# Spreading scale vectors by VectorE's stream shuffle and moving one batch's q load, in a fused attention and MLP kernel

## The chip, the cores and the metric

One core of a Trainium2 chip. The metric is the time of one execution on the device in microseconds. Every kernel was timed against the kernel before on the same chip in the same rounds. "The profile" is one profiled execution, with times from the start of its span (some 1.7 us shorter than the timed execution).

## The reference, cut to what matters

```python
# 8 batches, 16 q heads, 4 kv heads, 384 tokens, head size 64, so d_model = 1024
attn = softmax(q @ k.T / 8) @ v                 # then x: (8, 384, 1024)
a1 = alpha1 * x + beta1                         # vectors over d_model
u  = x + lam * einsum('ts,bsd->btd', w_tok, a1)
a2 = alpha2 * u + beta2
out = u + lam * (maximum(a2 @ w_ch1, 0) @ w_ch2)   # w_ch1 1024x4096, w_ch2 4096x1024
```

The kernel keeps w_ch2 in SBUF from the first batch on and streams w_ch1 (8 MB in bf16) anew for each batch. For each batch there are two channel passes: the first multiplies by w_ch1 (16 chunks of two 128-column tiles, matmuls "h"), the second by w_ch2 (matmuls "ch"). The attention of batch b+1 is woven into the second pass of batch b; that of batch 0 stands alone in the first 38 us, the attention stage.

## The kernel before: what the change and the argument touch

Four vectors of 1024 (alpha1 x lam, beta1 x lam, alpha2, lam) have to stand in all 128 partitions, in `vecs`. They come as rows of 32x128, are split into bf16 parts, and a PE matmul with a 0/1 weight adds the parts and spreads the sum:

```python
def spread(ps_, vs, tag, eng="DVE"):
    n = len(ps_)
    ps = bank([P, 4, P], tag, "vec")
    w = vs[1] - vs[0]
    for i, p in enumerate(ps_):
        nc.tensor.matmul(out=ps[:, i * w:(i + 1) * w], lhsT=sel[:, p:p + 1].to_broadcast([P, P]),
                         rhs=rows_b[:, vs[0] * P:vs[1] * P], start=True, stop=True)
    evac(eng)(out=vecs[:, vs[0]:vs[1], ...], in_=ps[:, :n * w]...)        # cut
```

The start, in GpSimd's order of issue (w1 tiles turn into bf16 on the way; a ring of five):

```python
load_v(0); load_q4(2); nc.gpsimd.dma_start(out=wtok_in, ...); load_q4(3)
place_k(0, 0, (0,))
load_w1(0); load_w1(1)
place_k(0, 1)
scale_rows(1, nc.gpsimd); split(1, 2, None, nc.gpsimd)
for c in range(2, RING):
    load_w1(c)
load_k(1); load_q(1); load_v(1)
for i in range(3):
    load_w2(0, i, 8)
for f in side(0):          # attention stage of batch 0
    f()
```

The end of the first channel pass, and where the third batch's q goes:

```python
if b or c + RING < NCH:
    load_w1(b * NCH + c + RING)          # tile of five chunks later
...
if b == 0 and c == NCH - 1:
    for i in range(RING):
        load_w1(NCH + i)
    load_next(2)                         # place_k(2), load_q(2), load_v(2)
...
moves = [(0, 1, flip_k, 2), (0, 1, flip_q, 2, 0, 2)] if b == 1 else []   # turns by DMA
turns = {16 + 8 * i: [(q_transpose, 2 + 2 * i, 2, "three")] for i in range(3)} if b == 2 else {}   # turns by PE
```

`side(b)` and `turns` hold what is woven in, by the number of steps that a pass has done (in the first pass four to a chunk, but two to each of the first two chunks of the first batch). A turn is a transposition, by DMA or by PE; a2T is the turned a2, which the matmuls "h" read. "tok" are the matmuls over w_tok, and R, in the tile `stage`, is a weight that they use in the first batch, made from the sums over w_tok.

The softmax here doesn't subtract the row's maximum and nothing guards it: scores larger than these inputs give would overflow.

## Time and profile before

| | before |
|---|---|
| median of the timed runs | 803.76 us (3 runs, 802.71 to 803.96) |
| profiled span | 802.3 us |
| PE busy | 790.1 us, 98% |
| first matmul of channel pass 1 of batch 0 (PE timeline) | 37.70 us |
| first matmul of its pass 2 | 77.61 us |
| first matmul of pass 1 of batch 1 | 132.66 us |
| first matmul of its pass 2 | 176.03 us |

The last four rows are milestones. They are starts of the first L414 or L447 matmul after the other one in PE's timeline.

### The profile page before, as it was taken

Reading aid. Unit: us, or ns where it says so; the run is one execution under the profiler, and the core shown is the slowest. Engines: PE = TensorE matmul, PEld = TensorE weight load, DVE = VectorE, ACT = ScalarE, POOL = GpSimd, SP = SyncE. Lnnn points to the kernel's source line nnn. Section 1 sums busy time; section 2 is a strip of 40 time slices with the busy share of each in tenths; the row PEclk is TensorE's granted clock in tenths of the full one; section 3 lists DMA queues with packets and bytes.
Section 4 is the critical chain, followed back from the end, with each engine's and each line's share of the span. In section 5 each row is a group of like instructions: output and inputs, shape, how many; then the busy total and the mean of one; then the engine's idle time right before and its main releaser. Section 6 shows DMA issues by size and latency. Waiting matters only on the chain.

```text
span 802.3 us, 14186 instructions
## 1 busy us (share of the span) xinstructions
PE 790.1 (98%) x6074; PEld 454.0 (57%) x6141; DVE 344.1 (43%) x667; ACT 226.6 (28%) x308; POOL 182.2 (23%) x241
## 2 busy tenths in 40 slices
PE   8999999999999999999999999999999999999997
PEld 5765555655556555565555655566555655556545
DVE  7652555226542256323662235622365225552122
ACT  7624331232412243123221234122431223312100
POOL 9234231342013500135002340033300330003000
PEclk9999999999999999999999999999999999999999
DMA  9999999998279962999339991499914994139511
GB/s 192 202 190 202 202 206 171 206 198 114 63 138 185 198 91 62 163 191 196 69 72 174 190 194 44 96 174 198 161 47 114 170 198 85 47 65 188 78 40 40
DMA packets 232575, 112.58 MB, mean 140 GB/s; under 512 B 81976, under 2 KB 226368, under 8 KB 232512
## 3 DMA queue, kind: packets, MB, share of 16 engines
q0 software_dynamic: 170752, 83.47, 78.9%
q1 hardware_dynamic: 61216, 27.81, 14.0%
q8 instruction: 48, 0.79, 0.4%
q10 hardware_dynamic: 544, 0.39, 0.2%
q14 instruction: 15, 0.12, 0.0%
HBM read 170.53 MB, written 12.58 MB: 228 GB/s over the span
## 4 chain that ended last, share of the span: by engine, by line
PE 96%; DVE 2%; issue 1%; DMA 1%; ACT 0%; SPq 0%
PE h L414 41%; PE ch L447 40%; PE sc L217 4%; PE sc L252 4%; PE sc L275 3%; DMA a2T<-a 1%; PE h L168 1%; PE tp L203 1%; PE tok L275 0%; PE av L252 0%; PE warm L464 0%; PE ut L292 0%; DVE x L258 0%; DVE x L282 0%; PE vec L332 0%
## 5 line engine op out<-in xcount | busy, mean ns | idle before, releaser
L447 PE MATMUL ch<-w,hT 128*128 128x512 bf16 (+2 forms) x1533 | 346.1, 370 | 4.4 <-issue 1.1
L414 PE MATMUL h<-a2T,w 128*128 128x384 bf16 (+1 forms) x2016 | 331.9, 326 | 0.5 <-DMA a2T<-a 0.4
L414 PEld LDWEIGHTS <-w 128*128 128x128 bf16 x2016 | 196.8, 98 | 130.2 <-issue 0.9
L134 POOL DMA_DIRECT2D w<-in_moe_w_ch_dram x128 | 112.2, 877 | 527.1 <-PE h L414 508.6
L447 PEld LDWEIGHTS <-hT 128*128 128x128 bf16 x1600 | 144.7, 98 | 152.6 <-issue 10.1
L226 ACT ACTIVATE es<-sc 128x1024 bf16<-128x1024 f32 x126 | 121.4, 1023 | 187.7 <-PE sc L217 178.8
L424 DVE TENSOR_SCALAR hT<-h,bias 128x384 bf16<-128x384 f32 x128 | 79.1, 618 | 216.0 <-PE h L414 215.4
L422 ACT ACTIVATE hT<-h,bias 128x384 bf16<-128x384 f32 x128 | 74.3, 580 | 304.6 <-PE h L414 304.0
L452 DVE TENSOR_TENSOR o<-ch,vecs 128x512 f32<-128x512 f32 (+2 forms) x50 | 33.5, 669 | 108.7 <-PE ch L447 108.7
L252 PEld LDWEIGHTS <-es 128*128 128x128 bf16 x1008 | 38.3, 97 | 13.2
L275 PEld LDWEIGHTS <-wtokT 128*128 128x128 bf16 x576 | 37.4, 98 | 12.3 <-DVE a L265 1.7
L217 PE MATMUL sc<-qT,kT 64*128 64x384 bf16 (+2 forms) x576 | 42.1, 272 | 1.3
L252 PE MATMUL sc<-v,es 128*128 128x65 bf16 x1008 | 39.8, 193 | 0.0
L257 DVE RECIPROCAL rinv<-sc 128x6 f32<-128x6 f32 x56 | 10.8, 194 | 67.4 <-PE sc L252 66.4
L282 DVE TENSOR_TENSOR x<-sc,x 128x384 f32<-128x384 f32 x56 | 31.0, 553 | 20.0 <-PE sc L275 20.0
L275 PE MATMUL sc<-a,wtokT 128*128 128x128 bf16 x504 | 37.3, 219 | 0.4
L217 PEld LDWEIGHTS <-kT 64*128 64x128 bf16 x576 | 21.7, 94 | 24.1 <-issue 19.1
L453 DVE TENSOR_TENSOR o<-o,x 128x512 f32<-128x512 f32 (+2 forms) x50 | 33.5, 671 | 1.7
L263 DVE TENSOR_TENSOR a1f<-x,vecs 128x384 f32<-128x384 f32 x56 | 31.4, 561 | 1.9
L265 DVE TENSOR_TENSOR a<-a1f,vecs 128x384 bf16<-128x384 f32 x56 | 31.4, 561 | 1.9
L286 DVE TENSOR_TENSOR a<-x,vecs 128x384 bf16<-128x384 f32 x56 | 31.3, 558 | 1.9
L258 DVE TENSOR_TENSOR x<-sc,rinv 128x384 f32<-128x384 f32 x56 | 31.2, 558 | 1.9
(80 smaller groups left out, 212.6 us busy)
## 6 DMA issues: line engine op xcount, KB each, us to landing
w<-in_moe_w_ch_dram POOLq DMA_DIRECT2D x144, 512.0 KB, 8.7
out_dram<-o SPq DMA_DIRECT2D x47, 256.0 KB, 2.2
q_raw<-in_q_dram POOLq DMA_DIRECT2D x28, 192.0 KB, 8.3
kst<-in_k_dram SPq DMA_DIRECT2D x16, 192.0 KB, 3.8
v<-in_v_dram POOLq DMA_DIRECT2D x24, 64.0 KB, 8.2
a2T<-a SPq DMA_TRANSPOSE x56, 2.3
qg<-in_q_dram POOLq DMA_DIRECT2D x3, 192.0 KB, 4.6
stage<-in_q_dram ACTq DMA_DIRECT2D x2, 192.0 KB, 3.7
```

Of the source, the lines that this page charges most:

```text
L134: nc.gpsimd.dma_start(out=t, in_=w1src[:, :, c * CW * P:(c + 1) * CW * P])
L217: nc.tensor.matmul(out=sc[:, hh, k % 4:k % 4 + n], lhsT=kT[r, sk, 2 * p // G, :], rhs=qT[r, p, st:st + n, :], start=True, stop=True)
L226: nc.scalar.activation(out=e, in_=sc, func=EXP, scale=scale_qk)
L252: nc.tensor.matmul(out=av[:, hh, sq, :], lhsT=ess[k // 4][:, m % 2, k % 4, :], rhs=vb[:, sk, hk, :], start=(sk == 0), stop=(sk == NST - 1))
L263: nc.vector.tensor_tensor(out=t, in0=x[:, :, cols(p)], in1=bc(g1, p), op=MUL)
L275: nc.tensor.matmul(out=ps[:, tt, :], lhsT=wtokT[:, st, tt * P:(tt + 1) * P], rhs=a1s[p][:, st, :], start=(st == 0), stop=(st == NST - 1 an ...
L414: nc.tensor.matmul(out=ps[:, :n], lhsT=w1[:, dt, j * P:(j + 1) * P], rhs=a2T[:, dt, :n], start=(dt == 0), stop=(dt == NDT - 1))
L422: nc.scalar.activation(out=hT[:, nt, :], in_=ps[:, :S], func=RELU, bias=c1)
L424: nc.vector.tensor_scalar(out=hT[:, nt, :], in0=ps[:, :S], scalar1=c1, scalar2=0.0, op0=ADD, op1=mybir.AluOpType.max)
L447: nc.tensor.matmul(out=ps[:, lo:hi], lhsT=hT[:, nt, ms * P:(ms + 1) * P], rhs=w2[:, nt, dw * 512 + lo:dw * 512 + hi], start=(nt == 0), sto ...
L452: nc.vector.tensor_tensor(out=o[:, lo:hi], in0=ps[:, lo:hi], in1=lam_t[:, c], op=MUL)
L453: nc.vector.tensor_tensor(out=o[:, lo:hi], in0=o[:, lo:hi], in1=x[:, ms, c], op=ADD)
```

## The change

Its intent: take the spread off PE, the bound engine, and keep the third batch's loads from delaying the last turns of batch 1. Vectors are loaded as float32 rows to partitions 0, 32, 64 and 96 and each group of 32 partitions copies its first row (`stream_shuffle`, mask 0). Cut to its core:

```diff
+        def load_vec(i, ap, lo, n):
+            nc.sync.dma_start(out=vecs[0:P:32, i, lo:lo + n], in_=bass.AP(..., ap=[[0, 4], [1, n]]))
+        def spread(i, half):
+            t = vecs[:, i, half * 512:(half + 1) * 512]
+            nc.vector.stream_shuffle(out=t, in_=t, mask=[0] * 32)
+        def scale(i, half, eng=nc.gpsimd):
+            t, m = (vecs[:, j, half * 512:(half + 1) * 512] for j in (i, 3))
+            eng.tensor_tensor(out=t, in0=t, in1=m, op=MUL)
 ...
         place_k(0, 0, (0,))
+        units = side(0)
+        for f in units[:8]:               # first scores, and spread(0, 0), spread(3, 0) on VectorE
+            f()
+        scale(0, 0)                       # GpSimd
         load_w1(0)
         load_w1(1)
         place_k(0, 1)
-        scale_rows(1, nc.gpsimd)
-        split(1, 2, None, nc.gpsimd)
-        for c in range(2, RING):
-            load_w1(c)
+        split()                           # GpSimd, one row set
+        nc.gpsimd.memset(stage[:, 2120:2824], 0.0)
+        nc.gpsimd.memset(vecs[:, 0:4:3, 512:], 0.0)
+        load_vec(0, moe_alpha1, 512, 512)
+        load_vec(3, moe_lam, 512, 512)
+        load_w1(2)
+        load_w1(3)
+        nc.gpsimd.memset(vecs[:, 1:3], 0.0)
+        load_w1(4)
         load_k(1)
+        load_vec(1, moe_beta1, 0, DM)
+        load_vec(2, moe_alpha2, 0, DM)
 ...
-              14: [(tok, 1), (ut, 0), (a1, 4)], 15: [(av, 5), ...
+              14: [(tok, 1), (spread, 0, 1), (spread, 3, 1), (scale, 0, 1, nc.vector), (ut, 0)], 15: [(a1, 4), (av, 5), ...
 ...
-                turns = {4: [(split, 2, 4, 0)], 8: [(split, 2, 4, 1)], ...   # and six PE spreads
+                turns = {4: [(spread, 1, 0)], 6: [(spread, 1, 1)], 8: [(scale, 1, 0), (scale, 1, 1), (spread, 2, 0)],
+                         10: [(spread, 2, 1)], ...
 ...
-            turns = {16 + 8 * i: [(q_transpose, 2 + 2 * i, 2, "three")] for i in range(3)} if b == 2 else {}
+            turns = {24 + 8 * i: [(q_transpose, 2 * i, 2, "three")] for i in range(4)} if b == 2 else {}
-                load_next(2)
+                place_k(2, 0)
+                place_k(2, 1)
+            if b == 1 and c in range(1, 5):
+                load_q(2, [G * (c - 1)])
+            if b == 1 and c == NCH - RING:
+                load_v(2)
-            moves = [(0, 1, flip_k, 2), (0, 1, flip_q, 2, 0, 2)] if b == 1 else []
+            moves = [(0, 1, flip_k, 2)] if b == 1 else []
```

## The prediction

> **What bounds the kernel now.** I read the page first: the busy shares, then the chain that ended last.
>
> ```profile
> PE 790.1 (98%) x6074; PEld 454.0 (57%) x6141; DVE 344.1 (43%) x667; ACT 226.6 (28%) x308; POOL 182.2 (23%) x241
> ...
> PE 96%; DVE 2%; issue 1%; DMA 1%; ACT 0%; SPq 0%
> ```
>
> The reader is to see that TensorE is the bound: busy 98% of the span, 96% of the chain. So the change can win only (a) PE instructions it takes away and (b) the few microseconds in which PE stands. The second view is the waits, for PE alone; these are all of them but those of its warm-up and issue.
>
> ```profile
> PE ch L447 <- DVE o L452: 0.9, 2, 0.5
> PE vec L332 <- DVE hT L540: 0.6, 1, 0.6
> PE h L414 <- DMA a2T<-a: 0.4, 1, 0.4
> ```
>
> The change touches the last two. The third view is the chain in order of time, at the start, where the scale rows are split into bf16 parts before PE may spread them:
>
> ```profile
> 8.99 1.03 DVE hT L534
> 10.02 0.02 issue
> 10.05 0.37 DVE hT L540
> 10.42 0.05 issue
> 10.46 0.40 PE vec L332 x4
> ```
>
> From 6.9 to 10.5 us the chain runs over VectorE's split, a real 3.6 us. But ScalarE's exponentials run beside it: the timeline shows them back to back from 8.15 to 11.00 and from 11.25 to 18.8 us, with 0.25 us between. The split is therefore not 3.6 us of loss.
>
> The fourth view is the timeline of PE in the first channel pass. It gives the price of a spread, the distance from one start to the next:
>
> ```profile
> 58.65 1.47 PE L414 MATMUL h<-a2T,w 128*128 128x385 bf16 x8
> 59.96 0.38 PE L332 MATMUL vec<-hT,stage 128*128 128x256 bf16 x2
> 60.18 2.78 PE L414 MATMUL h<-a2T,w 128*128 128x385 bf16 x16
> ```
>
> A spread there costs 60.18 - 59.96 = 0.22 us. Last I looked at what could newly bind, the transfers. These are GpSimd's timeline near the start and the issues of w1 tiles (512 KB each) to landing, for 37.5 to 38.2 us (the sixth tile, number 5) and 157 to 170 us (second batch's first pass):
>
> ```profile
> 7.10 1.82 POOL L134 DMA_DIRECT2D w<-in_moe_w_ch_dram  x2
> 13.89 2.74 POOL L134 DMA_DIRECT2D w<-in_moe_w_ch_dram  x3
> 37.83 1.75 POOL L134 DMA_DIRECT2D w<-in_moe_w_ch_dram  x2 [7.80 <-PE h L168]
> ...
> w<-in_moe_w_ch_dram POOLq DMA_DIRECT2D x1, 512.0 KB, 7.4
> ...
> w<-in_moe_w_ch_dram POOLq DMA_DIRECT2D x5, 512.0 KB, 8.1
> ```
>
> The page's slices show the DMA at 9 tenths and about 200 GB/s from the start to 120 us. In the second batch's first pass it moves 197 GB/s with w1 alone: 524 KB / 197 = 2.66 us for a tile, where PE uses one up in 2.60 us. So in these two passes the DMA is as full as PE, and only the ring of five tiles hides it.
>
> **What the Trainium skill says.** "VectorE: DVE Perf Modes", the perf-mode tier table: STREAM_SHUFFLE has only the 1x mode, some 2400 ns at 2048 elements. The same page's errata section gives (N+151)/0.96 ns for a float32 tensor_tensor, 691 ns at 512; the trace agrees (L452, 128x512 float32, median 691 ns). My estimate for a shuffle of 128x512 from these is 0.69 us; no run yet shows one. "GPSIMD Engine Reference", 3.1: a float32 tensor_tensor of 2048 takes 4497 ns on GpSimd; a quarter of that is 1.1 us, plus start-up I take 1.3 us for 128x512. The trace has only a 32x128 one, 0.45 to 0.57 us, which doesn't contradict it. "DMA: Bandwidth & Descriptors", "Issuing engines are not separate DMA queues": transfers issued from different engines share the same DMA engines, so a transfer moved to another place still takes from w1's. The trace agrees: with two k loads on the other queue at 138 us, landing of w1 went from 7.6 to 8.6 us.
>
> **The change part by part.**
>
> 1. *Spreads off PE.* In the first pass six spreads go: 6 x 0.22 = **-1.3 us**, wholly on the path if weights arrive. In the attention stage of batch 0 two go at 0.33 us (10.46 to 10.79, 19.32 to 19.65), and the 0.6 us wait before the first. There, PE waits for exponentials anyway. I add up ScalarE's gaps that the new order can close: 0.25 at 11.0, 0.28 at 18.8, 0.48 at 21.4, together about -1.0 us.
>
> 2. *VectorE instead.* At the start two shuffles (1.4 us) replace row scaling and split (6.89 to 10.42, about 2.9 us of work), and two PSUM copies (0.67 each) go. But at about 23 us two shuffles and a scale, 3 x 0.69 less overlap = 1.9 us, stand ahead of normalisations and the tok evictions. VectorE has no idle time from 20 to 26 us; with the 0.67 copy gone the delay is some 1.2 us, of which PE, with two buffers in PSUM, feels about 0.7. Stage sum: about -0.3 us. In the first pass four shuffles (2.8 us) take the place of 1.8 us of splitting; VectorE waits 1.4 to 2 us for PE in each chunk, so they are free.
>
> 3. *GpSimd's order.* GpSimd now waits for VectorE's shuffles (end about 8.2 us), scales (1.3 us), and only then issues the first two w1 tiles: 9.5 instead of 7.1 us. Next come the k copies (1.0), the row split (4.1 us in the old timeline, 9.76 to 13.89) and two new memsets. From the old 128x128 and 128x32 memsets (0.23 and 0.12 us) one element costs 1.15 ns, so 704 + 1024 elements take about 2.2 us. The third w1 tile is issued at about 18.8 instead of 13.9 us. The first two have landed by 19.0 (7.10 + 9.2 and 7.98 + 11.0), partly earlier now since the next batch's k loads also move behind the new small loads. The DMA, which never rested here, stands still for **2 to 3 us**. All later tiles shift by that. The sixth tile landed at 37.83 + 7.4 = 45.2 us and chunk 5 began at 45.85 (PE timeline: chunk 4 begins at 42.9 after four times 8 matmuls of 0.163 us from 37.7, plus 16 matmuls and one turn of 0.33): slack 0.65 us. So PE waits, and relative to before it is late by 2 to 3 less 0.65, **+2.0 us** taken. This swallows the gain of the attention stage: whatever PE wins before chunk 5, the tile's landing sets it. Later tiles had 0.7 to 2.2 us of slack, enough for the 1.3 us of part 1.
>
> 4. *q and v of the third batch* leave the first batch's second channel pass, where the last a2T turn waited behind them: the PE wait on a2T of 0.36 to 0.44 us goes, **-0.4 us**. They come to the second batch's first pass as four q loads of 192 KB behind tiles 6 to 9: about 1.0 us each at 190 to 197 GB/s, 4.1 us. The turn by DMA (some 0.9 us there, mostly before the tiles) goes; a fourth turn on PE comes, 16 matmuls apart as before: 0.33 us (144.48 to 144.81), **+0.3 us**. Slack of w1 in this pass, from issue plus landing against the start of the chunk: tile 6 1.4 us, tile 9 2.0, tile 10 149.83 + 8.5 = 158.3 against 160.2, about 2 (tiles numbered from 0 in the pass). The dips of the DMA between 138 and 142 us take in some 0.8. Left: 4.1 - 2 - 0.8, **+1.2 us** of PE wait around chunks 9 to 11.
>
> Sum: at chunk 5 +2.0 (stage 1 to 3), -1.3, -0.4, +0.3, +1.2 = **+1.8 us**. I shade it to +1.4, since the memsets and GpSimd's scale are only estimated: 805.2 us.
>
> **The rivals.** *A, the DMA keeps up.* If GpSimd is quicker than I think, or the rings hold enough, the attention stage may gain 0.65 (the slack of the sixth tile caps it), then -1.3, -0.4 and +0.3: -1.7, and 802.1 us. For it speaks that PE never waited for a w1 tile in the old trace; against it the 197 GB/s and the 0.65 us. *B, the weights bind more.* The DMA gap of 3 us and the whole 4.1 us of q beyond 2 of slack come through: +2.4 at chunk 5 and +2.1 in the second pass, with -1.4: +3.1, and 806.9 us; with a late upper half of the scale vectors (its load waits for the GpSimd memset, and VectorE waits in order) about 1 more, 808. *C, VectorE becomes the bound of the attention stage*: if a shuffle takes twice the estimate, four of them add 2.8 us to a stage in which it has no slack, perhaps 1.5 us at the end of the stage, but hidden under the same tile wait.
>
> **Range and chances.** A is the lower edge, B with the late half the upper: 802.0 to 808.0. 2% is 16 us, over twice anything above; only a wait that recurs in every batch could do it, and batches 3 to 7 are untouched. Faster 0.005, within 2% 0.98, slower 0.015.
>
> **What would show it.** Right: no PE time on a vec tile; shuffles of about 0.69 us; the third w1 issue near 18.8 us and low DMA share around 17 to 20 us; a PE wait on w1 of 1 to 2.5 us near 45 us and another near 155 to 162 us; no a2T wait at 134 us. Wrong: w1 issued before 16 us, no PE wait on w1 in either pass (then A), or a VectorE wait on vecs before 22 us that moves PE (then C).

## More of the kernel before

What the DMA does meanwhile, three stretches of 2 us (each row: stretch, length, then busy time and instruction count of PE, PE weight loads, VectorE, ScalarE, GpSimd; last three columns: PE clock, mean DMA share, GB/s):

```profile
16.00:18.00 2.00, 1.95 (x38) 1.35 (x36) 1.84 (x6) 2.00 (x4) 2.00 (x3) 1.00 1.46 199
18.00:20.00 2.00, 2.00 (x27) 1.02 (x24) 1.51 (x4) 1.72 (x3) 2.00 (x4) 1.00 1.45 197
20.00:22.00 2.00, 1.87 (x38) 1.51 (x37) 1.98 (x7) 1.52 (x3) 0.44 (x2) 1.00 1.46 198
```

The last column is what the reader should keep: 197 to 199 GB/s without a break.

## The result, and the profile after

The changed kernel took 808.71 us (median of 4 runs, 808.38 to 809.9) against 803.86 us in the same rounds. The ratio is 1.0064, 95% interval 1.0047 to 1.0081. (A ratio here is the mean time of one kernel's runs over that of the other's of the same rounds, so not quite the ratio of the medians.) It is slower by more than the noise, and 0.7 us above the upper edge of the predicted range.

First the chain that ended last (page of the changed kernel), then PE's waits in it (who waited for whom: total us, times, longest):

```profile
PE 88%; DMA 8%; POOL 2%; issue 1%; DVE 0%; POOLq 0%
```

```profile
PE h L400 <- DMA w<-in_moe_w_ch_dram: 4.2, 4, 2.3
...
PE tok L276 <- DVE x L259: 1.2, 1, 1.2
...
PE sc L218 <- ACT hT L227: 0.7, 2, 0.5
PE ch L438 <- DMA w<-in_moe_w_ch_dram: 0.5, 1, 0.5
PE tok L280 <- DVE stage L324: 0.5, 1, 0.5
PE h L400 <- DVE hT L410: 0.2, 1, 0.2
```

The chain now runs through transfers for 8% of the span, and PE, which had waited for no w1 tile before, waits for four. The a2T wait is gone. (Left out are the warm-up and an eviction of the last pass, both as before.) Next GpSimd's timeline, the cause of the first of the four:

```profile
8.36 1.27 POOL L522 TENSOR_TENSOR vecs<-vecs 128x512 f32<-128x512 f32 x1 [1.16 <-DVE vecs L518]
9.58 1.84 POOL L135 DMA_DIRECT2D w<-in_moe_w_ch_dram  x2
...
16.76 0.67 POOL L553 MEMSET stage<- 128x704 f32 x1
17.39 0.94 POOL L554 MEMSET vecs<- 128x1024 f32 x1
18.28 1.87 POOL L135 DMA_DIRECT2D w<-in_moe_w_ch_dram  x2
```

The third w1 issue comes at 18.28 us (before: 13.89). The sixth tile is issued at 38.64 us; from there it takes 10.7 us to landing, where it had taken 7.4 (GpSimd's timeline, then the issues from 38.6 to 39 us):

```profile
38.64 1.75 POOL L135 DMA_DIRECT2D w<-in_moe_w_ch_dram  x2 [3.30 <-PE h L169]
...
w<-in_moe_w_ch_dram POOLq DMA_DIRECT2D x1, 512.0 KB, 10.7
```

The same three stretches of the DMA as before:

```profile
16.00:18.00 2.00, 1.90 (x35) 1.46 (x34) 1.75 (x5) 2.00 (x3) 1.92 (x4) 1.00 1.07 141
18.00:20.00 2.00, 1.53 (x19) 0.81 (x17) 1.70 (x7) 1.67 (x4) 2.00 (x3) 1.00 0.04 8
20.00:22.00 2.00, 2.00 (x43) 1.74 (x42) 1.73 (x5) 1.44 (x3) 2.00 (x3) 1.00 1.07 121
```

8 GB/s where there had been 197. What PE makes of it, and two earlier waits (its timeline; start, duration, count, in brackets the wait):

```profile
26.18 0.34 PE L276 MATMUL tok<-hT,wtokT 128*128 128x128 bf16 x3 [1.23 <-DVE x L259]
...
42.74 2.13 PE L400 MATMUL h<-a2T,w 128*128 128x385 bf16 x12 [0.15 <-DVE hT L410]
...
45.05 2.12 PE L400 MATMUL h<-a2T,w 128*128 128x385 bf16 x12
49.43 0.83 PE L400 MATMUL h<-a2T,w 128*128 128x385 bf16 x4 [2.26 <-DMA w<-in_moe_w_ch_dram]
...
157.14 0.82 PE L400 MATMUL h<-a2T,w 128*128 128x384 bf16 x4 [0.40 <-DMA w<-in_moe_w_ch_dram]
...
160.79 2.77 PE L400 MATMUL h<-a2T,w 128*128 128x384 bf16 x16 [0.55 <-DMA w<-in_moe_w_ch_dram]
...
164.52 0.82 PE L400 MATMUL h<-a2T,w 128*128 128x384 bf16 x4 [0.95 <-DMA w<-in_moe_w_ch_dram]
```

A wait costs more than its bracket says, since the bracket counts from the modelled end of the matmul before. From start to start, 12 matmuls of 0.163 us from 45.05 end at 47.00, so 2.43 us are lost at 49.43; the three in batch 1 lose 0.57, 0.71 and 1.13 us in the same way, 2.41 in all. In the same way 0.33 us are lost at 42.74, where the eviction that PE waits for stood behind two shuffles, of which this is the second:

```profile
41.27 0.72 DVE L518 STREAM_SHUFFLE vecs<-vecs 128x512 f32<-128x512 f32 x1
```

The milestones, before and after, tell where the profiled spans differ (802.3 and 807.0 us):

| stretch | before | after | difference | of which |
|---|---|---|---|---|
| start to pass 1 of batch 0 | 37.70 | 38.50 | +0.80 | PE is 0.6 ahead near 24 us, then waits 1.2 us for VectorE at 26.18 |
| its pass 1 | 39.91 | 41.36 | +1.45 | sixth tile +2.43, VectorE's shuffles +0.33, six spreads -1.32 |
| its pass 2 | 55.05 | 55.58 | +0.53 | w2 wait of 0.47 (listed above) |
| pass 1 of batch 1 | 43.37 | 45.61 | +2.24 | w1 waits +2.41, turn +0.33, a2T wait -0.53 |
| the rest | 626.3 | 625.95 | -0.3 | |

The start has a scatter of its own. In the profiles of the kernel before and of its variants with an unchanged attention stage, the trace's record of the granted clock begins between 4.7 and 7.4 us, and pass 1 of batch 0 then starts between 36.4 and 37.7 us (the changed kernel's trace has no such record). Differences of up to 1.3 us there are to be taken with care, and the times of the kernel before scatter over 1.4 to 2.2 us for the same reason, I believe; five rounds average over it.

### The profile page after: what moved, and what is told of

The parts are those of the page before. It is cut to its first block, busy times and chain, and to the rows that moved or that the text cites.

```text
span 807.0 us, 14228 instructions
## 1 busy us (share of the span) xinstructions
PE 794.0 (98%) x6123; PEld 452.2 (56%) x6123; DVE 344.9 (43%) x669; ACT 223.0 (28%) x302; POOL 189.9 (24%) x247
## 4 chain that ended last, share of the span: by engine, by line
PE 88%; DMA 8%; POOL 2%; issue 1%; DVE 0%; POOLq 0%
PE ch L438 41%; PE h L400 35%; DMA w<-in_moe_w_ch_dram 6%; PE sc L218 4%; PE sc L253 4%; PE sc L276 3%; DMA q_raw<-in_q_dram 1%; POOL w L135 1%; PE warm L455 0%; PE tp L204 0%; POOL w L140 0%; POOL vecs L559 0%; POOL q_raw L117 0%; DVE vecs L518 0%; POOL hT L530 0%
## 5 line engine op out<-in xcount | busy, mean ns | idle before, releaser
L438 PE MATMUL ch<-w,hT 128*128 128x512 bf16 (+2 forms) x1600 | 357.6, 371 | 1.4 <-DVE o L443 0.9
```

The lines of the kernel that those rows point to most:

```text
L438: nc.tensor.matmul(out=ps[:, lo:hi], lhsT=hT[:, nt, ms * P:(ms + 1) * P], rhs=w2[:, nt, dw * 512 + lo:dw * 512 + hi], start=(nt == 0), sto ...
```

## The experiments

The theory after the result has three parts. G: GpSimd's new order holds the w1 issues back, the transfers lose time near 18 us, and the sixth tile comes late. Q: the third batch's q takes transfer time from w1 in a pass that has none to spare. V: the upper half's shuffles stand in VectorE's way in the attention stage. The rival is that shuffles as such, or the small vector loads, cost the time. Eleven kernels ran, each in 5 rounds (one in 6).

### Each half by itself

The second half undone in the changed kernel (the last part of the diff above reversed):

> The changed kernel with only its second half undone: the third batch's q and v are loaded at the end of the first channel pass and turned as before. Theory Q (q in the second pass holds up w1 there): the three waits for w1 between 156 and 165 us (0.57 + 0.71 + 1.13 us from start to start, 2.4 in all) go, one PE turn (0.33) goes, the a2T wait (0.5) comes back: 2.2 us faster than the change, about 806.5. The wait of about 2.4 us at 47 us stays. Rival (the loss in the second pass is carried over from the transfer gap at 17 us): the second pass keeps its waits and the time stays within 0.7 us of 808.7.

And only that half, on the kernel before:

> The kernel before with only the second half of the change: q and v of the third batch in the second pass. Theory Q: no a2T wait at 134 us (-0.5), a fourth turn (+0.33), waits for w1 of about 2.4 us around 155 to 165 us: +2.2 us against before, about 806. Rival (it hurts only together with the first half's late transfers): 803.5 to 804.2.

Measured: e1 806.62 us, ratio 1.0040 (1.0027 to 1.0052); e2 806.32 us, ratio 1.0029 (1.0016 to 1.0042). In e1 the three late waits are gone and one of 1.9 us near 49 us stays, with an a2T wait of 0.2; in e2 it is the other way round, three w1 waits of 0.86, 0.58 and 0.93 us between 153 and 162 us and no other. The halves add: 0.40% and 0.29% against 0.64% for both. Theory Q and the split in two hold; the rivals of both expectations fall.

### GpSimd's order alone

```diff
+        load_w1(0)
         scale(0, 0)
-        load_w1(0)
         load_w1(1)
         place_k(0, 1)
+        load_w1(2)
+        load_w1(3)
         split()
 ...
-        load_w1(2)
-        load_w1(3)
-        nc.gpsimd.memset(vecs[:, 1:3], 0.0)
         load_w1(4)
+        nc.gpsimd.memset(vecs[:, 1:3], 0.0)
```

> The changed kernel with GpSimd's order alone altered: the first w1 tile issued before the scale, tiles 2 and 3 before the row split, tile 4 before the last memset. Theory G (GpSimd holds back the issues, the transfers stand still at 17 to 21 us): the third w1 issue comes near 12.4 us, the DMA does not pause, the wait for w1 at 47 us (2.4 us) goes; VectorE's fill may wait some 0.6 us for the later split and memset. 2 to 2.5 us faster than the change, about 806.4. Rival (the shuffles or the small vector loads themselves slow the stage): no more than 0.5 us faster.

Measured: 808.43 us, ratio 1.0061 (1.0047 to 1.0075); four runs of 808.3 to 809.1, one, the profiled, of 806.72. In the profile the DMA moves 195 and 206 GB/s from 16 to 24 us and the wait at 49 us is gone, as G has it. But the split, now after the issues, lets VectorE wait 1.31 us for the memset and PE 1.33 us for VectorE, another 1.78 us at 26.77 (1.23 in the changed kernel), and pass 1 starts at 39.09 instead of 38.50 us. What it won in one place it lost in another, so by the median this run is a miss. The four slower runs have a mean clock of 0.997 to 0.998, the fast one 1.0 (the changed kernel's three runs with a clock of 1.0 took 808.38 to 808.82). What a fallen clock costs is told below; at which wait it fell in these four is not known, since only the fast one was profiled.

### The gap without the change

Three memsets of vectors that are not filled yet, on GpSimd in the kernel before (2048, 2048 and 1024 elements), ahead of the third w1 issue:

```diff
         split(1, 2, None, nc.gpsimd)
+        nc.gpsimd.memset(vecs[:, 1:3], 0.0)
+        nc.gpsimd.memset(vecs[:, 1:3], 0.0)
+        nc.gpsimd.memset(vecs[:, 3], 0.0)
         for c in range(2, RING):
```

> The kernel before with nothing of the change, but three memsets on GpSimd (some 4.6 us by the changed kernel's own, 1.84 for 2048 elements) ahead of the third w1 issue. Theory G: the issue moves from 13.9 to 18.5 us, the DMA pauses 2.5 to 4 us from about 18 us, PE waits for the sixth w1 tile near 46 us some 2 to 3 us: 805.9 to 806.8. Rival (what costs in the change is the shuffles on VectorE or the vector loads): 803.9 as before.

Measured: 806.46 us, ratio 1.0036 (1.0024 to 1.0049). The issue moved to 18.87 us, the DMA moved 13 GB/s from 18 to 20 us and 73 from 20 to 22. G is confirmed without a single shuffle. Its profiled run was its slowest (807.89 us) and shows a second cost. PE's timeline:

```profile
48.20 0.83 PE L414 MATMUL h<-a2T,w 128*128 128x385 bf16 x4 [3.48 <-DMA w<-in_moe_w_ch_dram]
...
49.29 4.37 PE L414 MATMUL h<-a2T,w 128*128 128x385 bf16 x16
...
53.83 2.78 PE L414 MATMUL h<-a2T,w 128*128 128x385 bf16 x16
```

and the stretches around it (third column from the right: the granted clock of TensorE):

```profile
48.00:49.00 1.00, 0.80 (x7) 0.54 (x8) 0.00 (x0) 0.00 (x0) 0.00 (x0) 1.00 1.46 199
49.00:50.00 1.00, 1.00 (x10) 0.65 (x8) 0.47 (x1) 0.00 (x0) 0.00 (x0) 0.55 1.45 196
50.00:51.00 1.00, 1.00 (x5) 0.49 (x4) 0.09 (x1) 0.16 (x1) 0.00 (x0) 0.50 1.45 198
...
53.00:54.00 1.00, 1.00 (x13) 0.73 (x11) 0.78 (x2) 0.00 (x0) 0.70 (x1) 1.00 1.46 199
```

The same 16 matmuls take 4.37 instead of 2.78 us: after the wait the clock is halved for 3.41 us (the trace's record), and 1.6 us more are lost. The other four runs have a clock of 1.0 and lie near 806.3. Such runs (0.997 or 0.998) also turn up in the changed kernel (809.9 us) and in every experiment in which PE waits long (most often in e3, e8 and e11), never in the runs of the kernel before (0.999 at least). They lie within 1.5% of the fastest; their cost is part of the medians and ratios given here.

### Half the gap

One memset of 2048 elements instead of the three.

> The kernel before with one memset of 2048 elements (1.8 us) on GpSimd ahead of the third w1 issue, where the run with the gap had three (4.5 us). Theory (the transfers' pause counts, not the delay of the issue): issue near 16.2 us, full rate some 2.7 us after an issue into an empty queue as in the run with the gap, so near 18.9 us where the queue ran dry near 17.9: a pause of about 1 us, PE waits 0.4 us at most for the sixth tile, 803.8 to 804.4. Rival (each microsecond of delayed issue costs its share): 1.8/4.5 of 2.5 us, 804.9.

Measured: 805.06 us, ratio 1.0016 (1.0003 to 1.0029); the profiled run, the slowest of the five (807.44), has a wait of 1.95 us for the sixth tile and a halved clock after it, so its losses are likely above those of the others. The issue came at 15.93 us and the DMA never stood still. Yet it moved 141, 175, 135 and 180 GB/s in the four stretches of 2 us from 18 to 26 us, where it had moved about 198. Summed from 16 to 38 us (11 stretches) that is 0.40 MB less than before, 2.05 us at 197 GB/s, and the sixth tile landed 2.3 us later (47.5 against 45.2). In e4 the same sum is 0.72 MB less, 3.7 us. My expectation fell, and its rival (804.9) came near: not the standstill counts but every lost microsecond of transfer, and a queue that only nearly runs dry loses too. Why the rate stayed low for so long after 18 us is open.

Counted from the start of the span, the transfers tell more. The sixth tile lands once 8.8 to 8.9 MB have been moved: 8.81 before (at 45.2 us), 8.77 in e4 (48.1), 8.94 in e9 (47.5), 8.87 in the changed kernel (49.3). At 38 us the changed kernel is 0.90 MB behind (6.46 against 7.36), and 0.33 MB of that was lost before 16 us, where nothing stood still but the first two w1 tiles had been issued 2.5 us later. In e4, where those two are issued as before, only 0.03 MB is missing at 16 us.

### The upper half's shuffles taken away

```diff
-              14: [(tok, 1), (spread, 0, 1), (spread, 3, 1), (scale, 0, 1, nc.vector), (ut, 0)], ...
+              14: [(tok, 1), (ut, 0)], ...
```

> The changed kernel without the two shuffles and the scale of the vectors' upper half at 23 us (a wrong result on purpose). Theory: they make PE wait 1.23 us for VectorE at 25 us, so the first channel pass begins 1.2 to 1.5 us earlier, near 37.2 us; but the sixth w1 tile lands when it did (49.3 us), the wait for it grows from 2.3 to about 3.5 us, and the whole is no faster than the change: 808.7, or slower by up to 1.7 if the longer wait lets the TensorE clock fall as in the run with the gap alone. Rival (the two losses add): 1.2 us faster, 807.5.

Measured: 809.42 us, ratio 1.0069 (1.0057 to 1.0082), result wrong as intended. Pass 1 starts at 36.68 us, 1.8 us earlier (up to 1.3 us of it may be the scatter of the start: the clock's record begins at 4.8 us here), and PE no longer waits for `x` of VectorE. It then waits longer for the same tile, though that came 1.0 us earlier than in the changed kernel:

```profile
48.45 0.83 PE L400 MATMUL h<-a2T,w 128*128 128x385 bf16 x4 [3.10 <-DMA w<-in_moe_w_ch_dram]
...
49.71 4.19 PE L400 MATMUL h<-a2T,w 128*128 128x385 bf16 x16
```

In four of five runs the clock fell (0.998); the one with a clock of 1.0 took 808.42, against 808.38 to 808.82 of the changed kernel. So work off the path was taken away and the kernel became no faster, which is V's place in the sum: hidden under the tile.

### q spread over more chunks

```diff
-            turns = {24 + 8 * i: ...            # the turns on PE
+            turns = {24 + 10 * i: ...
 ...
-            if b == 1 and c in range(1, 5):
-                load_q(2, [G * (c - 1)])
+            if b == 1 and c in range(1, 8, 2):
+                load_q(2, [G * (c // 2)])
```

> The changed kernel with the four q loads of the second pass after chunks 1, 3, 5 and 7, where it had 1, 2, 3 and 4 (PE turns at chunks 6, 8, 11 and 13). Theory (the DMA is full in this pass, every byte more delays w1): the waits come later, but sum to nearly as much, 1.8 to 2.5 us: 808.2 to 808.9. Rival (the burst of four loads outruns the ring, spread out they fit): waits under 0.8 us, 807 or less.

Measured: 808.25 us, ratio 1.0061 (1.0049 to 1.0073). The waits came at 160, 167 and 173 us, of 0.53, 0.96 and 0.65 us: 2.1 listed, where the changed kernel had 1.9. So the bytes cost, and not their coming in a burst.

### q at the end of the second pass: two tries

In the order of issue alone (`load_next(2)` cut to the k copies, `load_q(2)` and `load_v(2)` after the last turn of the second pass), on the kernel before:

> The kernel before, but q and v of the third batch are issued at the very end of the second channel pass of batch 0 (after its last a2T turn), not at the start of that pass. If the a2T wait of 0.5 us came from these loads, it goes, and w1 in the next pass is not held up since the DMA stood idle there from 131 to 136 us: 0.5 us faster than before, 803.4. If the loads now run into w1 of the next pass as in the changed kernel, up to 2 us slower.

Measured: 803.75 us, ratio 1.0000 (0.9987 to 1.0012). This tested nothing: GpSimd waits for nothing at that place, ran ahead, and issued the loads when it had before (the last v load at 122.4 us, before at 123.3). Yet the a2T wait is absent from its profile, as it is from those of e4, e6 and e9, all with these loads in their old place; in e1 it is 0.24 us. So the wait comes and goes without the loads being moved, and that they cause it is not shown. An instruction is late only if something makes it wait. So a second version makes GpSimd copy one element that VectorE writes after the last tok of the pass, into the tile that q goes to:

```diff
+        nc.gpsimd.tensor_copy(out=qrs[b][:, 0, 0, 0:1], in_=xs[b - 1][:, 0, DM - 1:DM])
         for h in range(0, Hq, G):
```

> The kernel before, with the third batch's q and v really held back: GpSimd first copies an element that VectorE writes after the last tok of the second channel pass (the earlier try moved only the place in GpSimd's order, and GpSimd, waiting for nothing, issued them at 104 us as before). q issued after 128 us. If these loads cause the a2T wait: none at 134 us (-0.5), q lands by about 137 us, no new wait for w1: 803.3. If they now meet w1 of the next pass: 804 to 805.

Measured: 807.12 us, ratio 1.0043 (1.0031 to 1.0055). The loads were issued from 128.3 us on and there is no a2T wait, but PE waits 1.54 and 1.01 us for w1 at 146.81 and 150.59 us, and four of six runs show a fallen clock; the two with a clock of 1.0 took 805.55 and 806.06. That is worse than either case I had expected. The 0.5 us of the a2T wait, where it comes at all, is a cheap price for the early place.

### The shuffle where there is room

The kernel before with PE's early spread of the first vector kept; the other three vectors loaded to four partitions and shuffled in the first channel pass, one shuffle to a chunk; their memset on GpSimd after all early w1 and w2 issues:

```diff
+        nc.gpsimd.memset(vecs[:, 1:4], 0.0)      # after load_w2(0, i, 8)
+        load_vec(1, moe_beta1); load_vec(2, moe_alpha2); load_vec(3, moe_lam)
 ...
-                turns = {4: [(split, 2, 4, 0)], 8: [(split, 2, 4, 1)], ...   # and six PE spreads
+                for i in range(6):
+                    turns[36 + 4 * i] = [(shuffle, (1, 3, 2)[i // 2], i % 2)]
+                for i in range(2):
+                    turns[50 + 4 * i] = [(scale, 1, i)]                       # on VectorE
```

> The kernel before with PE's early spread of the first vector kept, but the other three vectors loaded to four partitions after all early w1 issues and spread by VectorE's shuffle in the first channel pass. If what costs in the change is only the place (GpSimd's order and VectorE in the attention stage), and PE really gives back 6 x 0.22 us: 1.3 us faster than before, 802.6, no wait for w1 over 0.5 us. If a shuffle in the pass holds up PE (0.33 us seen in the changed kernel): 803. If shuffles as such are the cost: 804 or more.

Together with the edit of e5:

> Both of the former together. The gains add if they lie in different stages: 1.8 us faster than before, 802.1. If the start of the ring in the second pass now binds: 802.6 to 803.4.

Measured: e6 803.02 us, ratio 0.9985 (0.9972 to 0.9999); e7 802.27 us, ratio 0.9981 (0.9968 to 0.9993). Pass 1 of batch 0 takes 38.64 and 38.60 us instead of 39.91: the 1.3 us of the six spreads are real. In neither profile does the a2T wait appear. All that the view of who waited for whom lists for PE in e7 is this:

```profile
PE warm L465 <- DVE wtokT L468: 1.5, 1, 1.5
PE vec L332 <- DVE hT L541: 1.1, 1, 1.1
PE ch L448 <- DVE o L453: 0.9, 2, 0.5
```

e7 beats both kernels: the kernel before by 0.2%, the changed one by 0.8% (by the medians, of different rounds). As its edit of q did nothing to the times of issue in e5, I take e6 and e7 for nearly the same kernel; that e6 has a w2 wait of 0.7 us and e7 none is not explained. The rival that shuffles as such cost the time falls.

## Why the prediction was wrong, point by point

The mechanism stood: off PE 1.3 us, into transfers more than that. Several sizes did not, the two that decided it both in the transfers, and the total came 0.7 us above the upper edge. Two sums are also off: rival A's terms give -2.05 (801.7 us), not -1.7, and 4.1 - 2 - 0.8 is 1.3, not 1.2; neither explains the miss.

- *"Spreads off PE", -1.3 us.* Right: 39.91 to 38.60 us in e7.
- *"VectorE instead", stage sum about -0.3 us.* Wrong: +0.80 in the profile. I put PE's part of VectorE's delay at 0.7 us; the wait is 1.23. Of the gains that I added for ScalarE's gaps about half came (its first twelve exponentials end at 18.28 us, before at 18.82); then PE, earlier at tok, waited 0.5 us for the eviction of R, and 1.23 us as above. Shuffles in the pass, "so they are free", cost 0.33 us where two come between two of VectorE's evictions; one to a chunk, in e6 and e7, costs nothing. By e8 the stage's loss was hidden anyway.
- *"GpSimd's order".* The third issue was foreseen at 18.8 us and came at 18.28; the scale took 1.27 us, not 1.3, the two memsets 1.61, not 2.2. The step that failed is "The DMA, which never rested here, stands still for 2 to 3 us. All later tiles shift by that". The sixth tile landed at 38.64 + 10.7 = 49.3 us, 4.1 us later than before. Two terms were left out. One is the running dry and the start of a dry queue: after the issue at 18.28 us the rate stayed at 0 until 19.5 us and the full rate of about 200 GB/s only near 21.5 us, so that from 16 to 22 us 0.65 MB is missing, 3.3 us at 197 GB/s. The other is the slower transfer before 16 us, 0.33 MB or 1.7 us (a part of both was made up later). e9 adds that a queue that nearly runs dry pays too. In place of +2.0 us at chunk 5 stand 0.80 + 0.33 + 2.43 = 3.56; with 4.1 for the shift, my own sum would have given 4.1 - 0.65 = 3.45.
- *"q and v of the third batch".* +0.3 for the turn was right. -0.4 for the a2T wait agrees with the profiles (-0.53 from start to start), but by luck as far as is known: the wait is also missing in e4, e5, e6 and e9, which leave these loads where they were. The step that failed is "The dips of the DMA between 138 and 142 us take in some 0.8": in place of +1.2 us the waits were 2.41. Without that credit the sum would have been 4.1 - 2 = 2.1. The trace agrees: in the changed kernel the dip is still there (147 and 75 GB/s in the two microseconds from 140 us), and the first q load is issued only after it, at 142.42 us. e10 shows that spreading the loads over more chunks does not buy it back.
- *Not foreseen*: a w2 wait of 0.47 us in pass 2 of batch 0, +0.53 with what goes with it. No run isolates its cause. The late w1 alone is not it: e4 and e9 have that and no such wait, while e6, with w1 in time, has one of 0.71 us. It appears only in kernels without the six spreads on PE (also e1 and e10), but not in all of them.
- *Shading.* I took the sum of +1.8 down to 1.4 since durations of GpSimd were estimated. They were near enough (the third issue came 0.5 us before its estimate); what should have been doubted was the recovery of the DMA, and that points up. My rival B, 806.9 to 808 us, was the likelier case, and its cap too low.
- *Rival C* came true as a wait of VectorE but not as a cost: e8.

## What to carry to other kernels

An instruction on the engine that issues transfers costs nothing only as long as the queue behind it stays full: look at the GB/s of the stretch before putting work ahead of an issue, and count the refill of an empty queue. Where PE and DMA are both full, bytes moved into a pass come back as PE waits, less what the ring holds in reserve (here 2.41 us of 4.1), and what is won before such a wait is lost in it. Moving an instruction in a queue's order moves nothing in time if it waits for nothing; and the way to use the shuffle here was to keep its gain (1.3 us of PE) and put its memsets and loads after the issues that matter.

## What the Trainium skill lacked or had wrong

- "VectorE: DVE Perf Modes", perf-mode tier table, has a duration of a shuffle for 2048 elements only. From its figures I had estimated 0.69 us for a float32 shuffle of 128x512, which is near: the runs show 0.72 us each, 0.63 from one start to the next of two in a row, and a mask load of 0.01 before each.
- "GPSIMD Engine Reference" has no figure for a memset (what 3.1 states of a tensor_tensor, 4497 ns at 2048 elements, fits: a quarter of it is 1.12 us, and the runs show 1.27 for 128x512); the runs show 0.67, 0.94 and 1.84 us for 704, 1024 and 2048 float32 elements in each of 128 partitions.
- "DMA: Bandwidth & Descriptors", Latency and other measured facts, gives about 1 us for the first byte of a transfer issued by GpSimd; here it was 1.1 us in e4 (18.87 to 20.0). It has no figure for how long an emptied queue takes to its full rate: here some 3.2 us from the issue (18.28 to 21.5 us in the changed kernel, 18.87 to 22.0 in e4; the 2.7 us in my expectation of e9 was read too low). Nor does it tell of the low rate of a queue that nearly runs dry (135 to 180 GB/s over 8 us in e9).
- "TensorE: Matmul & The Clock Gate", Part 1, has the clock fall after an idle window of about 3.4 us. In these runs PE did not have to stand for a whole window. The halved stretch lasted 3.41 us in e4, e8 and e9, and the record of full clock before it 13, 13 and 12 times as long (44.37, 44.37 and 40.96 us). If stretches of 3.41 us are laid out from the start of each record, PE stood for 2.52, 2.71 and 1.95 us of the one just before the fall. The most in any stretch without a fall, in the profiles of this case that have such a record, is 1.86 us (e1). Two kernels with like waits can thus differ by how a wait lies in this grid. For the 2.26 us of the changed kernel's profiled run, after which the matmuls went on at 0.163 us each, this cannot be looked up, since its trace has no record of the clock.
